# Attention and MLP on one core: batch 0's loads split in the order of use, batch 2's reordering moved up to right behind the GELU pass

## The chip, the cores and the metric

One core of a Trainium2 chip. The time is that of one execution on the device, in microseconds (us); a kernel is compared with the kernel before by runs on the same chip in the same rounds.

## The reference

Softmax attention with one added to the denominator, then a two-layer MLP with exact GELU on its rows:

```python
batch, n_heads, seq, head_dim = (8, 12, 448, 64)
scores = scale * q @ k.T
e = exp(scores - max(scores))
attn = e / (sum(e) + exp(-max) + 1e-09)
x = concat_heads(attn @ v)                 # 3584 rows of 768
h = x @ w_in                               # w_in 768 x 2048
out = (0.5 * h * (1 + erf(h / sqrt(2)))) @ w_out
```

## The kernel before

The kernel works in 48 steps, one for each pair of heads of each batch (6 pairs in a batch). A step makes scores on TensorE, exponentials on ScalarE (ACT), sums of exponentials on VectorE (DVE), then values and denominators on TensorE for a pair one to three steps back. From the seventh step on MLP work of the batch before fills TensorE. GpSimd (POOL) issues all loads but the first four, SyncE (SP) the DMA transposes and most stores.

Queries and keys are needed with head_dim on the partitions. For batches 0 and 1 TensorE transposes them; from batch 2 on DMA does. Batch 2 comes as heads and is first reordered into pairs by VectorE.

```python
raw_pool = ctx.enter_context(tc.tile_pool(name="raw_pool", bufs=2))
ps_bank  = ctx.enter_context(tc.tile_pool(name="ps_bank", bufs=2, space=PSUM))
...
def order_by_pairs(b, w, c0, c1):
    n, nj, raw, name = ((PS, NJ, q_raw, "rawq"), (P, NK, k_raw, "rawk"))[w]
    if b not in ordered[w]:
        ordered[w][b] = raw_pool.tile([n, H, nj, D], FP16, name=name)
    src = raw[b].rearrange("p (c e) j d -> p c e j d", e=2)
    dst = ordered[w][b]...("p (c j e d) -> p c j e d", c=NPAIR, j=nj, e=2)
    for e in range(2):
        nc.vector.tensor_copy(out=dst[:, c0:c1, :, e, :], in_=src[:, c0:c1, e])   # L258
```

The buffers of one name are given out in turn.

```python
def start_step(s):                     # steps 0 to 5
    ...                                # scores, normalize(s - 2)
    transpose_on_pe(0, s + 1)          # pair s + 1 of batch 0
    for c in {NPAIR - 2: (0,), NPAIR - 1: (1, 2, 3)}.get(s, ()):
        transpose_on_pe(1, c)          # batch 1's pairs 0 to 3; pair 4 in step 6
    ...                                # scores of the left-over keys, values, denominators, logarithm
...
step(NPAIR + 1, mlp1(0, 2, 6))
gelu_window(0, 6)
for s in range(NPAIR + 2, NSTEP + 1):
    b, r = divmod(s - 2 - NPAIR, NPAIR)
    ...
        step(s, take(n), ...)          # r == 0: one half of layer 2, evicted by VectorE (osb, L457)
    if b == 0 and r == 0:
        transpose_on_pe(1, NPAIR - 1)  # batch 1's last pair
    fetch(b, r)                        # reordering and DMA transposes
```

Steps count from 0 in the code, so `start_step(0)` is the first step. To evict is to copy a result out of the memory that TensorE writes to (PSUM); `ps_bank` has two such buffers, and a bank is free for the next result only after its eviction.

The softmax here doesn't subtract the row's maximum and nothing guards it: scores larger than these inputs give would overflow.

Of the kernel before, what the change touches and what calls it, by code (L numbers as in the profile page):

```python
# [9 lines left out]
FP32 = mybir.dt.float32  # L10
FP16 = mybir.dt.float16
# [8 lines left out]
def kernel(  # L20
# [9 lines left out]
    nc = tc.nc  # L30

    B, H, S, D = q.shape
    DM = H * D
    DFF = moe_w_in.shape[1]
    P = 128
# [3 lines left out]
    NPAIR = H // 2  # L39
# [4 lines left out]
    LEFT = S % P  # L44
# [7 lines left out]
    shift = math.log(float(S + 1))  # L52

    const = ctx.enter_context(tc.tile_pool(name="const", bufs=1))
# [16 lines left out]
    def load_table(set_id):  # L71
        nc.scalar.add_instruction(  # L72
            mybir.InstLoadActFuncSet(
                name=nc.get_next_instruction_name(),
                act_func_set_id=set_id,
                engine=mybir.EngineType.Activation,
                ins=[],
                outs=[],
            )
        )  # L80
# [6 lines left out]
    kl_raw = [left_pool.tile([P, NPAIR, P], FP16, name=f"klraw{i}") for i in range(2)]  # L87
    vl = [left_pool.tile([P, NPAIR, P], FP16, name=f"vl{i}") for i in range(2)]
    q_raw, k_raw, v_t, qt_t = {}, {}, {}, {}

    def load_heads(tiles, pool, name, src, b, h0=0, h1=H):

        n, nj = (PS, NJ) if src is q else (P, NK)
        if b not in tiles:
            tiles[b] = pool.tile([n, H, nj, D], FP16, name=name)
        nc.gpsimd.dma_start(  # L96
            out=tiles[b][:, h0:h1],
            in_=src[b, h0:h1, 0:n * nj].rearrange("h (p j) d -> p h j d", j=nj),
        )
# [12 lines left out]
    def load_left(tiles, src, b):  # L112
        view = src[b, :, NFULL:S].rearrange("(c e) s d -> e s c d", e=2)
        for e in range(2):
            nc.gpsimd.dma_start(  # L115
                out=tiles[b % 2][e * LEFT:(e + 1) * LEFT, :, e * D:(e + 1) * D], in_=view[e])

    def load_q(b, *heads):
        load_heads(q_raw, raw_pool, "rawq", q, b, *heads)

    def load_k(b, *heads):
        load_heads(k_raw, raw_pool, "rawk", k, b, *heads)

    def load_v(b, *heads):
        load_heads(v_t, v_pool, "vn", v, b, *heads)
# [34 lines left out]
            load_table(SET_LN_EXP)  # L160
    ident = const.tile([P, P], FP16, name="ident")
    make_identity(nc, ident)
    for t in (kl_raw[1], kl_raw[0], vl[0], vl[1]):
        nc.vector.memset(t, 0.0)
    load_left(kl_raw, k, 0)
    load_q(0, 4, 6)
    load_k(0, 4, 6)

    warm = ps_bank.tile([P, 512], FP32, name="bank")
    for _ in range(7):  # L170
        nc.tensor.matmul(
            warm, kl_raw[1][:, 0], kl_raw[1].rearrange("p c x -> p (c x)")[:, 0:512],
            start=True, stop=True)
    ones = const.tile([P, D], FP16, name="ones")
    nc.vector.memset(ones, 1.0)
    ones_left = const.tile([P, P], FP16, name="ones_left")
    nc.gpsimd.memset(ones_left, 0.0)
    for e in range(2):
        r = slice(e * LEFT, (e + 1) * LEFT)
        nc.gpsimd.memset(ones_left[r, e * D:(e + 1) * D], 1.0)  # L180
    expb = const.tile([P, 1], FP32, name="expb")
    nc.vector.memset(expb, -shift)
    oneb = const.tile([P, 1], FP32, name="oneb")
    nc.vector.memset(oneb, math.exp(-shift))

    load_v(0, 0, 6)
    load_left(vl, v, 0)
    load_q(0, 6, 12)
    load_k(0, 6, 12)
    load_v(0, 6, 12)  # L190
    load_q(1)
    load_k(1)
    load_left(kl_raw, k, 1)
# [209 lines left out]
    def layer1(b, fc, direct=False, mid=None):  # L403
        ph = ps_bank.tile([P, 512], FP32, name="bank")
        for m in range(MCH):
            matmul_cols(
                ph[:, 0:S], w_in_sb[:, m, fc * P:(fc + 1) * P], xt_t[b][:, m, :],
                m == 0, m == MCH - 1)
        if mid:
            mid()  # L410
        if direct:
            for c0, c1, dst in gelu_out(b, fc, fc + 1):
                nc.scalar.activation(out=dst[:, 0, :], in_=ph[:, c0:c1], func=AF.Gelu)  # L413
        else:
            if fc == 0:
                h_t[b] = h_pool.tile([P, NBURST, S], FP32, name="hbuf")
            nc.vector.tensor_copy(out=h_t[b][:, fc, :], in_=ph[:, 0:S])  # L417

    def gelu_burst(b, f0, f1):
        for c0, c1, dst in gelu_out(b, f0, f1):  # L420
            nc.scalar.activation(out=dst, in_=h_t[b][:, f0:f1, c0:c1], func=AF.Gelu)
# [15 lines left out]
    def layer2_items(b):  # L437
        if b % 2 == 0:
            tiles = [(gt_even, t * P, [(b, t * P, (t + 1) * P)]) for t in range(NFULL // P)]
        else:  # L440
            tiles = [(gt_odd, 0, [(b - 1, NFULL, S), (b, 0, LEFT)])]
            tiles += [(gt_odd, (t + 1) * P, [(b, LEFT + t * P, LEFT + (t + 1) * P)])
                      for t in range(NFULL // P)]
        halves = []
        for gt, g0, where in tiles:
            def half(nh, mid=None, gt=gt, g0=g0, where=where):

                n0 = nh * NHW
                po = ps_bank.tile([P, 512], FP32, name="bank")
                for fc in range(FCH):  # L450
                    matmul_cols(
                        po[:, 0:NHW], gt[:, fc, g0:g0 + P], w_out_sb[:, fc, n0:n0 + NHW],
                        fc == 0, fc == FCH - 1)
                    if mid and fc == FCH // 2 - 1:
                        mid()
                osb = osb_pool.tile([P, NHW], FP32, name="osb")
                nc.vector.tensor_copy(out=osb, in_=po[:, 0:NHW])  # L457
                r0 = 0
                for bb, c0, c1 in where:
                    store_cols(osb, r0, bb, c0, c1, n0)  # L460
                    r0 += c1 - c0

            for nh in range(NH):
                halves.append((nh if b == 0 else 0, lambda mid=None, nh=nh, half=half: half(nh, mid)))
        return [f for _, f in sorted(halves, key=lambda x: x[0])]
# [75 lines left out]
    def mlp1(b, f0, f1):  # L541
        return [lambda mid=None, fc=fc: layer1(b, fc, mid=mid) for fc in range(f0, f1)]

    def take(n):
        got = l2[:n]
        del l2[:n]
        return got

    def gelu_window(b, n):

        load_table(SET_GELU)
        ready = take(len(l2))
        for f in ready:
            f()
        if not ready:
            for i in range(FCH - n):
                if i < n:
                    gelu_burst(b, i, i + 1)
                layer1(b, n + i, direct=True)
        else:  # L560
            for f0 in range(0, n, n // 2):
                gelu_burst(b, f0, f0 + n // 2)
            for fc in range(n, FCH):
                layer1(b, fc, direct=True)
        load_table(SET_LN_EXP)
        l2.extend(layer2_items(b))
# [34 lines left out]

    def fetch(b, r):

        if r == 0 and b + 2 < B:
            load_v(b + 2)
            load_left(vl, v, b + 2)
        if b == 0 and r in (0, 2):
            c0 = 0 if r == 0 else NPAIR // 2
            for w in range(2):
                order_by_pairs(2, w, c0, c0 + NPAIR // 2)  # L610
                transpose_on_dma(2, w, c0, c0 + NPAIR // 2)
        elif b and r in (0, 1) and b + 2 < B:
            transpose_on_dma(b + 2, r)
        if r == 3 and b + 3 < B:
            load_pairs(q_raw, "rawq", q, b + 3)
            load_pairs(k_raw, "rawk", k, b + 3)
            load_left(kl_raw, k, b + 3)

    step(NPAIR + 1, mlp1(0, 2, 6))
    gelu_window(0, 6)  # L620
    for s in range(NPAIR + 2, NSTEP + 1):
        b, r = divmod(s - 2 - NPAIR, NPAIR)

        half = NBURST // 2
        if b and r < 2:
            step(s, mlp1(b, half * r, half * (r + 1)))
        else:
            left = len(l2) - (0 if b == 0 else 1 if b % 2 == 0 else 2)
            n = left if r == NPAIR - 1 else max(1, left // (NPAIR - r))
            if b and r == 2:  # L630
                n = 2
            step(s, take(n), late=(s == NSTEP or r == (2 if b else 0)))
        if b == 0 and r == 0:
            transpose_on_pe(1, NPAIR - 1)
        fetch(b, r)
        if b and r == 1:
            gelu_window(b, 2 * half)
# [43 lines left out]
```

## Time and profile before

| | |
|---|---|
| time, median | 415.83 us (three runs); 415.61 with a fourth |
| TensorE busy | 400.3 of 414.9 us |
| its idle time from 5 to 40 us | 7.9 us |
| its longest waits for data | 1.7 + 1.1 us (pair 3's queries and keys), 0.7 us (batch 2's transposes) |

TensorE is full from 40 us to near the end, so a change has to take idle time away ahead of that or at 76 us. The lines are in the prediction below. Two marks make runs comparable. One is the table load that opens the first GELU pass on ScalarE, the other the first exponentials of the step near 92 us.

In the timeline of the kernel before (start, length, engine, line, what, then idle time before it and who ended it):

```profile
43.06 1.28 ACT L72 ACT_TABLE_LOAD   x1
...
76.33 0.74 PE L315 MATMUL st<-tqk 64*128 64x448 f16 x6 [0.72 <-DMA tqk<-rawk]
...
92.47 3.33 ACT L305 ACTIVATE et<-st,expb 128x896 f16<-128x896 f32 x4 [2.22 <-PE st L315]
```

The first mark is at 43.06, the second at 92.47, 49.41 us later; the 0.72 us that TensorE waits for batch 2's transposes lie between.

### The profile page before, as it was taken

The numbers are of one execution on the slowest core, as the hardware profiler recorded it, in microseconds if no ns is written. First come the engines' busy times: TensorE is split into PE (matmuls) and PEld (weight loads), VectorE is DVE, ScalarE is ACT, GpSimd is POOL, SyncE is SP. The second block draws the span as 40 slices with busy tenths as digits, with TensorE's granted clock in tenths as the row PEclk, the third lists the DMA queues.
The fourth block names the chain that finished last, engine by engine and source line by source line (L and its number), as shares of the span: only waits on it lengthen the run. The fifth ranks groups of instructions, "written<-read, shape, count | busy, mean of one in ns | idle before, by whom it ended". The sixth has DMA issues, their size and how long they took to land.

```text
span 414.9 us, 10361 instructions
## 1 busy us (share of the span) xinstructions
PE 400.3 (97%) x4403; PEld 249.9 (60%) x4403; DVE 194.8 (47%) x466; ACT 300.5 (72%) x450; POOL 101.5 (24%) x138
## 2 busy tenths in 40 slices
PE   7779999999999999999999999999999999999996
PEld 3345765556656565566555566556565565687785
DVE  5466428773266713674165722576046741540021
ACT  6798879979897757979687766997589676734300
POOL 8631330773523450054300651020000000000000
PEclk9899999999999999999999999999999999999999
DMA  9999999999983997199921999149211100110022
GB/s 154 181 201 202 197 201 178 154 183 162 136 102 67 152 177 65 58 91 140 151 60 44 140 144 118 56 71 136 63 40 42 35 23 20 45 54 20 2 77 76
DMA packets 136638, 43.76 MB, mean 105 GB/s; under 512 B 117712, under 2 KB 136592, under 8 KB 136592
## 3 DMA queue, kind: packets, MB, share of 16 engines
q0 software_dynamic: 91408, 22.39, 57.7%
q1 hardware_dynamic: 43952, 19.60, 29.0%
q10 hardware_dynamic: 1232, 1.11, 0.9%
q8 instruction: 34, 0.56, 0.6%
q14 instruction: 12, 0.10, 0.1%
HBM read 45.61 MB, written 11.01 MB: 136 GB/s over the span
## 4 chain that ended last, share of the span: by engine, by line
PE 88%; DMA 4%; ACT 4%; POOL 2%; DVE 1%; issue 0%
PE bank L224 71%; PE st L315 6%; PE bank L363 6%; DMA tqk<-rawk 3%; ACT et L305 2%; DMA rawk<-in_k_dram 2%; PE st L224 2%; PE st L371 2%; ACT rec L380 1%; ACT rec L383 1%; DVE xt L389 0%; POOL klraw L115 0%; POOL vl L115 0%; POOL rawq L96 0%; ACT L72 0%
## 5 line engine op out<-in xcount | busy, mean ns | idle before, releaser
L305 ACT ACTIVATE et<-st,expb 128x896 f16<-128x896 f32 x192 | 160.3, 914 | 34.7 <-PE st L315 26.0
L224 PE MATMUL bank<-xt,w_in_sb 128*64 128x448 f16 x1536 | 152.4, 353 | 0.2
L224 PEld LDWEIGHTS <-w_in_sb 128*64 128x64 f16 x1536 | 92.8, 110 | 55.6 <-issue 6.3
L457 DVE COPY osb<-bank 128x384 f32<-128x384 f32 x56 | 31.2, 557 | 123.5 <-PE bank L224 123.5
L224 PE MATMUL bank<-w_out_sb,gt_odd 128*64 128x384 f16 x1024 | 88.2, 327 | 0.0
L224 PEld LDWEIGHTS <-gt_odd 128*64 128x64 f16 x1024 | 60.8, 110 | 25.5 <-issue 4.5
L224 PE MATMUL bank<-w_out_sb,gt_even 128*64 128x384 f16 x768 | 68.9, 327 | 0.0
L389 DVE TENSOR_TENSOR xt<-bank,rec 128x448 f16<-128x448 f32 x48 | 29.7, 619 | 64.6 <-PE bank L363 56.0
L224 PEld LDWEIGHTS <-gt_even 128*64 128x64 f16 x768 | 43.6, 110 | 22.9 <-issue 4.4
L413 ACT ACTIVATE gt_odd<-bank 128x448 f16<-128x448 f32 (+1 forms) x74 | 29.1, 394 | 23.0 <-PE bank L224 21.9
L417 DVE COPY hbuf<-bank 128x448 f32<-128x448 f32 x54 | 33.6, 623 | 16.5 <-PE bank L224 15.2
L110 POOL DMA_DIRECT2D rawq<-in_q_dram x40 | 30.7, 783 | 37.2 <-DVE rawq L258 17.0
L315 PE MATMUL st<-tqk 64*128 64x448 f16 x288 | 36.9, 353 | 2.8 <-ACT et L305 1.0
L363 PE MATMUL bank<-et,vn 128*64 128x448 f16 x288 | 36.3, 357 | 0.0
L349 DVE TENSOR_TENSOR ksum<-t,et 128x448 f16<-128x448 f16 x96 | 33.9, 384 | 0.8 <-ACT et L305 0.6
L349 DVE TENSOR_TENSOR t<-et 128x448 f16<-128x448 f16 x96 | 33.2, 388 | 2.1 <-ACT et L305 0.8
L413 ACT ACTIVATE gt_even<-bank 128x384 f16<-128x384 f32 x34 | 16.7, 490 | 22.1 <-PE bank L224 22.1
L349 DVE TENSOR_TENSOR ksum<-ksum,et 64x448 f16<-64x448 f16 x84 | 31.9, 380 | 1.3
L96 POOL DMA_DIRECT2D vn<-in_v_dram x9 | 8.8, 981 | 89.6 <-PE st L315 86.8
L110 POOL DMA_DIRECT2D rawk<-in_k_dram x30 | 24.7, 824 | 20.6 <-DMA rawq<-in_q_dram 19.8
L380 ACT ACTIVATE rec<-st,oneb 128x448 f32<-128x448 f32 x42 | 27.1, 647 | 2.8 <-PE st L371 2.8
L383 ACT ACTIVATE rec<-rec 128x448 f32<-128x448 f32 x48 | 27.6, 577 | 1.5
(57 smaller groups left out, 234.5 us busy)
## 6 DMA issues: line engine op xcount, KB each, us to landing
vn<-in_v_dram POOLq DMA_DIRECT2D x7, 576.0 KB, 10.2
rawq<-in_q_dram POOLq DMA_DIRECT2D x40, 84.0 KB, 11.1
w_in_sb<-in_moe_w_in_dram POOLq DMA_DIRECT2D x4, 768.0 KB, 19.8
w_out_sb<-in_moe_w_out_dram POOLq DMA_DIRECT2D x4, 768.0 KB, 19.8
rawk<-in_k_dram POOLq DMA_DIRECT2D x31, 96.0 KB, 7.4
out_dram<-osb SPq DMA_DIRECT2D x16, 168.0 KB, 2.3
out_dram<-osb SPq DMA_DIRECT2D x16, 144.0 KB, 2.1
out_dram<-osb SPq DMA_DIRECT2D x16, 120.0 KB, 2.0
```

Of the source, the lines that this page charges most:

```text
L110: nc.gpsimd.dma_start(out=dst[:, :, j, e, :], in_=view[j, e])
L224: nc.tensor.matmul(out[x], lhs[:, x], rhs, start=start, stop=stop)
L305: nc.scalar.activation(out=out, in_=in_, func=AF.Exp, bias=expb, scale=scale)
L315: nc.tensor.matmul(st[:, e, 0:S], kt[r, j, :], qt[r], start=True, stop=True)
L349: nc.vector.tensor_tensor(out=dst, in0=a, in1=x, op=ALU.add)
L363: nc.tensor.matmul(po_t[g][e * D:(e + 1) * D, 0:S], v_t[b][:, 2 * c + e, j, :], et[:, 2 * j + e], start=False, stop=(j == NK - 1),)
L380: nc.scalar.activation(out=rec_t[g], in_=den_t.pop(g)[:, 0:S], func=AF.Ln, bias=oneb, scale=1.0)
L383: nc.scalar.activation(out=rec_t[g], in_=rec_t[g], func=AF.Exp, scale=-1.0)
L389: nc.vector.tensor_tensor(out=xt_t[b][:, c, :], in0=po_t.pop(g)[:, 0:S], in1=rec_t.pop(g), op=ALU.mult)
L413: nc.scalar.activation(out=dst[:, 0, :], in_=ph[:, c0:c1], func=AF.Gelu)
L417: nc.vector.tensor_copy(out=h_t[b][:, fc, :], in_=ph[:, 0:S])
L457: nc.vector.tensor_copy(out=osb, in_=po[:, 0:NHW])
```

## The change

It splits batch 0's later loads so that pair 3's queries and keys come alone and first. It starts GpSimd's queue earlier, with a shorter form of warm-up. It moves the reordering of batch 2's first half ahead of the ninth step (s = 8 in the code), so that its DMA transposes go out earlier; the load of batch 2's values is written two steps later.

```diff
-    for t in (kl_raw[1], kl_raw[0], vl[0], vl[1]):
+    nc.vector.memset(ones, 1.0)
+    for t in (kl_raw[0], vl[0], kl_raw[1], vl[1]):
         nc.vector.memset(t, 0.0)
-    nc.gpsimd.memset(ones_left, 0.0)          # and two more
+    nc.vector.memset(ones_left, 0.0)          # and two more
-    for _ in range(7):
-        nc.tensor.matmul(warm, kl_raw[1][:, 0], <512 columns of kl_raw[1]>, ...)
+    for _ in range(54):
+        nc.tensor.matmul(warm[0:D, 0:D], ones, ones, start=True, stop=True)
-    load_v(0, 0, 6)
+    load_v(0, 0, 4)
     load_left(vl, v, 0)
-    load_q(0, 6, 12)
-    load_k(0, 6, 12)
-    load_v(0, 6, 12)
+    load_q(0, 6, 8)
+    load_k(0, 6, 8)
+    load_q(0, 8, 12)
+    load_k(0, 8, 12)
+    load_v(0, 4, 12)
 ...
-        if r == 0 and b + 2 < B:
+        if r == (0 if b else 2) and b + 2 < B:
             load_v(b + 2)
             load_left(vl, v, b + 2)
-        if b == 0 and r in (0, 2):
-            c0 = 0 if r == 0 else NPAIR // 2
+        if b == 0 and r in (-1, 2):
+            c0 = NPAIR // 2 if r == 2 else 0
 ...
     gelu_window(0, 6)
+    fetch(0, -1)
```

More of the change, by code (lines that the diff above doesn't have):

```diff
@@ L162 @@
     make_identity(nc, ident)
-    for t in (kl_raw[1], kl_raw[0], vl[0], vl[1]):
+    ones = const.tile([P, D], FP16, name="ones")
+    nc.vector.memset(ones, 1.0)
+    for t in (kl_raw[0], vl[0], kl_raw[1], vl[1]):
         nc.vector.memset(t, 0.0)
+    ones_left = const.tile([P, P], FP16, name="ones_left")
+    nc.vector.memset(ones_left, 0.0)
+    for e in range(2):
+        r = slice(e * LEFT, (e + 1) * LEFT)
+        nc.vector.memset(ones_left[r, e * D:(e + 1) * D], 1.0)
+    expb = const.tile([P, 1], FP32, name="expb")
+    nc.vector.memset(expb, -shift)
+    oneb = const.tile([P, 1], FP32, name="oneb")
+    nc.vector.memset(oneb, math.exp(-shift))
     load_left(kl_raw, k, 0)
@@ L169 @@
     warm = ps_bank.tile([P, 512], FP32, name="bank")
-    for _ in range(7):
-        nc.tensor.matmul(
-            warm, kl_raw[1][:, 0], kl_raw[1].rearrange("p c x -> p (c x)")[:, 0:512],
-            start=True, stop=True)
-    ones = const.tile([P, D], FP16, name="ones")
-    nc.vector.memset(ones, 1.0)
-    ones_left = const.tile([P, P], FP16, name="ones_left")
-    nc.gpsimd.memset(ones_left, 0.0)
-    for e in range(2):
-        r = slice(e * LEFT, (e + 1) * LEFT)
-        nc.gpsimd.memset(ones_left[r, e * D:(e + 1) * D], 1.0)
-    expb = const.tile([P, 1], FP32, name="expb")
-    nc.vector.memset(expb, -shift)
-    oneb = const.tile([P, 1], FP32, name="oneb")
-    nc.vector.memset(oneb, math.exp(-shift))
-    load_v(0, 0, 6)
-    load_left(vl, v, 0)
-    load_q(0, 6, 12)
-    load_k(0, 6, 12)
-    load_v(0, 6, 12)
+    for _ in range(54):
+        nc.tensor.matmul(warm[0:D, 0:D], ones, ones, start=True, stop=True)
+    load_v(0, 0, 4)
+    load_left(vl, v, 0)
+    load_q(0, 6, 8)
[3 more added lines that the diff above has]
+    load_v(0, 4, 12)
     load_q(1)
```

## The prediction

> **What bounds the kernel now.** I read the page first: busy shares and slices, to see whether there is anything to win and where.
>
> ```profile
> PE 400.3 (97%) x4403; PEld 249.9 (60%) x4403; DVE 194.8 (47%) x466; ACT 300.5 (72%) x450; POOL 101.5 (24%) x138
> ...
> PE   7779999999999999999999999999999999999996
> ...
> PEclk9899999999999999999999999999999999999999
> ```
>
> TensorE is busy 400.3 of 414.9 us, so all its idle time is 14.6 us. The busy time by stretch puts it: about 1.5 us before 5 us, 6.7 from 5 to 30 us (the fourth digit is the last below 9), 1.2 from 30 to 40, 1.1 from 60 to 80, and 4.1 in the last 15 us, which the change doesn't touch. What the change can win is therefore a part of some 9 us, 2.2% of the time; over 2% faster is out of reach. The second thing to see is the clock digit 8 in slice 2 (10.4 to 20.7 us): half speed for about 3 us (finer windows: 0.65 at 16.0 to 16.5, 0.50 from 16.5 to 19.5).
>
> Next, the waits of TensorE:
>
> ```profile
> PE bank L232 <- DMA rawq<-in_q_dram: 1.7, 1, 1.7
> ...
> PE bank L237 <- DMA rawk<-in_k_dram: 1.1, 1, 1.1
> ...
> PE st L315 <- DMA tqk<-rawk: 0.7, 1, 0.7
> ```
>
> The first two are one place: transposes of head pair 3 wait for queries and keys of heads 6 to 11, which come in one load each. The third is batch 2, whose first scores wait for its DMA transposes. The change aims at these. The timeline (start, length, engine, idle before and who ended it) of that place and of the same spot two steps on:
>
> ```profile
> 14.99 0.40 PE L232 MATMUL bank<-ident,rawq 112*64 112x112 f16 x8 [1.69 <-DMA rawq<-in_q_dram]
> 16.52 0.54 PE L237 MATMUL bank<-ident,rawk 128*64 128x128 f16 x6 [1.13 <-DMA rawk<-in_k_dram]
> 17.70 1.34 PE L363 MATMUL bank<-et,vn 128*64 128x448 f16 x6
> 19.77 0.63 ACT L380 ACTIVATE rec<-bank,oneb 128x448 f32<-128x448 f32 x1 [1.56 <-PE bank L224]
> 20.92 3.31 ACT L305 ACTIVATE et<-st,expb 128x896 f16<-128x896 f32 x4
> 25.27 3.31 ACT L305 ACTIVATE et<-st,expb 128x896 f16<-128x896 f32 x4
> ...
> 26.27 0.37 PE L237 MATMUL bank<-ident,rawk 128*64 128x128 f16 x6
> 26.44 0.26 PE L242 MATMUL bank<-ident,klraw 128*64 128x128 f16 x2
> ```
>
> After the wait the values matmuls run at half clock (1.34 us for six here, 0.77 for the same six a step later). Away from the wait ScalarE sets the pace: its steps begin at 20.92 and 25.27, 4.35 us apart, with no idle time.
>
> Last, the loads (from issue to landing, the last figure), asked one by one:
>
> ```profile
> rawq<-in_q_dram POOLq DMA_DIRECT2D x1, 336.0 KB, 7.3
> rawk<-in_k_dram POOLq DMA_DIRECT2D x1, 288.0 KB, 8.1
> vn<-in_v_dram POOLq DMA_DIRECT2D x1, 288.0 KB, 10.1
> rawk<-in_k_dram POOLq DMA_DIRECT2D x1, 576.0 KB, 14.7
> klraw<-in_k_dram POOLq DMA_DIRECT2D x1, 48.0 KB, 14.0
> ```
>
> Issued at 7.64, 8.40, 9.22, 10.97 and 11.97, they land at 14.9, 16.5, 19.3, 25.7 and 26.0; the second klraw load at 26.4. So batch 1's keys and left-over keys land just as TensorE reads them (26.27, 26.44). That is the fact my number hangs on: the queue is full, and a second wait stands right behind the one removed.
>
> **What the Trainium skill says.** "TensorE: Matmul & The Clock Gate", Part 1: the array runs at half clock until busy for a window of about 3.4 us, and falls back after an idle one, the windows running free. The trace agrees: half clock from about 16.4 to 19.5, 3.1 us, after two waits. The same section gives N / 1.2 GHz from start to start of cold matmuls; the 7 warm-up ones of 512 columns fit (3.17 us for all, 0.43 each). "DMA: Bandwidth & Descriptors", Anatomy of one DMA, has a fixed cost of about 2 us for a gpsimd load; the two small loads at 3.42 and 4.08 (3.8 and 3.5 us to landing, some 0.7 of it issue) don't contradict it. Its Specifications want 512 B a descriptor for full rate; the query rows are 512 B, the key and value rows 384, the left-over rows 128, and the queue moves 150 to 210 GB/s here.
>
> **The change part by part.**
>
> 1. Start of GpSimd's queue. The tile that the first left-over load waits for is cleared second of its list instead of after the other: one memset of 0.38 less, less 0.06 for `ones`, so the load starts about 0.3 us earlier than 2.00. The three `ones_left` memsets go from GpSimd to VectorE: the values load starts right after the key load instead of at 5.39 after a stretch of 0.6. In all, values are issued about 0.9 us earlier, and the hole in the traffic at 7 to 8 us (64 against 165 GB/s around it, worth 0.6 us) mostly closes. VectorE's own list ends by about 3.0 us, before its first cast at 4.16.
>
> 2. Warm-up: 54 matmuls of 64 columns for 7 of 512: 3456 columns for 3584, from 1.0 instead of 1.34. At the skill's cold rate an estimate is 54 x 53 ns = 2.9 us, ending near 4; TensorE next works at 4.64. If a weight load doesn't hide behind so short a matmul they take up to twice that and push the start by a microsecond or so. I give nothing for this part.
>
> 3. Order of loads. Before pair 3's keys lie 96+112+96+288+96+336+288 = 1312 KB; after, 96+112+96+192+96+112+96 = 800 KB. 512 KB at about 190 GB/s is 2.7 us, with the earlier start over 3: they land near 13 instead of 16.5, and TensorE asks at 13.3. The wait and the half clock go. ScalarE's step 3 then begins at 13.93 + 4.35 = 18.28 instead of 20.92: 2.64 us won so far. Values of heads 4 to 11 keep the byte count ahead of them, land near 18.7, and are wanted near 19.7: no wait.
>
> 4. What gives it back. Bytes ahead of batch 1's keys and left-overs are the same, so these land earlier only by part 1, which I take as 0.7: 25.7 for the last. TensorE would now ask at 26.44 - 2.64 = 23.8 and wait. From the left-over transposes to the end of the denominators is 28.03 - 26.44 = 1.6 us, so step 4's logarithm can begin at 25.7 + 1.6 = 27.3, against 28.45 before: **1.15 us** remain of 2.64. From there to 60 us all runs on as before, shifted: input weights land at 30.2 to 41.5, against first use at 36.4 and, for the last quarter, about 52.
>
> 5. Batch 2. Four copies (1.00 + 0.80 us of VectorE) move from 62.4 into VectorE's gap between 46.8 and 59.9; their data land at 55.4 and 56.9 before, so the transposes go out at about 56 instead of 63.5. They took 10.4 and 10.6 us to land (73.9 and 76.3); even at 13 they are there by 72. The wait of **0.7** goes. GpSimd's list of operations is the same from here on: values come behind the second half of keys in it either way, so "two steps later" moves no issue. Stores behind the transposes on SyncE's queue come late, but four output buffers cover three steps.
>
> Sum: 1.15 + 0.72 = 1.9 us, from 415.83 to 413.9. I take off little more than a tenth of that for the risks below and say 414.1.
>
> **The rivals.** (a) The second wait takes all: TensorE idles about 2 us near 24, its clock drops as it did at 16.4, and den-to-logarithm takes 2.9 instead of 1.6. For: the same shape of wait did just this. Against: the idle is shorter than the 2.8 before. One chance in four; then only some 0.5 us is won, 415.3. (b) No second wait, since the loads come much earlier: 2.64 + 0.7 = 3.4 us, 412.5. Against: the queue is full from 8 us on. One in seven. (c) The earlier DMA transposes slow batch 2's second-half loads (landing at 67.0 and 69.2, wanted on VectorE at 72.2 and 73.1). Putting the rest of about 0.8 MB ahead of them costs an estimated 2 to 3 us at 200 GB/s, about the margin. VectorE would then hold up the next step by under a microsecond: 414.8. (d) The warm-up is too long or doesn't lift the clock: 1 us lost; one in ten.
>
> **Range and chances.** Center 414.1; (b) gives the low end, 412.6, (a) with (d) the high end, 415.6. The whole idle time in reach (9 us) is just over the 8.3 us that 2% asks, and no part here risks 8 us: faster 0.01, same 0.98, slower 0.01.
>
> **What would show it.** The query and key waits near 14 to 16.5 are gone and the clock stays full there (3); a new wait of TensorE on batch 1's keys or left-over keys near 24 to 25.7, with ScalarE's step 5 at about 28.5 for 29.62 (4); the first DMA transposes issued near 56 and no wait for them at the scores near 75 (5); first scores still near 5.9 (2). Wrong if that second wait is missing or costs the clock, or if VectorE waits for batch 2's second half.

## The result and the profile after

The changed kernel took 416.44 us (median of four, 415.99 to 417.37), against 415.61 before. The ratio is 1.0023, 95% interval 1.0001 to 1.0045. Ratios here are the mean time of one kernel's fast runs over that of the other's of the same rounds, so not quite the ratio of the medians. It is slower by 0.2%, and the predicted range ended at 415.6. The interval only just leaves out 1, and a control with identical code (e8, below) gave nearly as large a ratio, so the loss itself is hardly shown; what is shown is that the predicted win did not come.

The page of the changed kernel, busy shares and slices:

```profile
PE 399.9 (96%) x4450; PEld 252.1 (61%) x4450; DVE 195.5 (47%) x469; ACT 300.5 (72%) x450; POOL 102.3 (25%) x137
...
PE   7789979999999999999999999999999999999996
...
PEclk9999999999999999999999999999999999999999
```

The clock digit 8 is gone (PEclk is the share of full speed granted to TensorE, in tenths), the third slice has 8 for 7, and there is a new 7: slice 6, 51.9 to 62.2 us. The waits of TensorE in the changed kernel (total us, times, longest) name it:

```profile
PE bank L224 <- DVE osb L457: 3.0, 1, 3.0
```

Its timeline shows how it comes about, on VectorE:

```profile
58.50 1.01 DVE L258 COPY rawq<-rawq 112x768 f16<-112x768 f16 x2 [14.43 <-PE bank L232]
59.43 0.80 DVE L258 COPY rawk<-rawk 128x576 f16<-128x576 f16 x2
60.15 0.78 DVE L349 TENSOR_TENSOR ksum<-ksum,et 64x448 f16<-64x448 f16 x2
60.94 0.56 DVE L457 COPY osb<-bank 128x384 f32<-128x384 f32 x1
```

and on TensorE:

```profile
58.06 0.39 PE L232 MATMUL bank<-ident,rawq 112*64 112x112 f16 x8
...
61.64 0.38 PE L224 MATMUL bank<-et,vl 128*64 128x448 f16 x2 [2.96 <-DVE osb L457]
```

VectorE sits idle for 14.43 us in front of the first copy, although the queries are there from about 54.0 us and the keys from 55.6. What ends the wait is the query transposes of batch 1's last pair, which start at 58.06 and take 0.39 us. Only then can the copies run, 1.8 us of them; the sums behind them take 0.8; and the first output eviction, ready since about 57.9, begins at 60.94. TensorE needs the bank that it empties and waits 2.96 us. The wait that the move was to take away did go: the DMA transposes went out at 59.61 and 61.92 us and had landed by 74.7, so TensorE does not wait for them.

The two marks of the changed kernel, and one step in between:

```profile
27.60 3.31 ACT L305 ACTIVATE et<-st,expb 128x896 f16<-128x896 f32 x4
...
41.04 1.28 ACT L72 ACT_TABLE_LOAD   x1
...
92.51 3.33 ACT L305 ACTIVATE et<-st,expb 128x896 f16<-128x896 f32 x4 [2.22 <-PE st L315]
```

The first mark comes at 41.04 for 43.06: 2.02 us won ahead of the GELU pass, in this pair of traces. From there to the second it takes 51.47 us for 49.41: 2.06 us lost. In these two traces the sum is zero. In the medians it is 0.8 us of loss, because the profile of the kernel before had fallen on a slow execution: that execution took 416.62 us, 0.8 to 1.0 over the kernel's median, while the profiled run of the changed kernel (416.6) lies near its own.

### The profile page after: what moved, and what is told of

The parts are those of the page before. It is cut to its first block, busy times and chain, and to the rows that moved or that the text cites. A ratio compares the mean times of both kernels' runs of the same rounds, so it can differ in the third digit from the quotient of the medians.

```text
span 414.8 us, 10457 instructions
## 1 busy us (share of the span) xinstructions
PE 399.9 (96%) x4450; PEld 252.1 (61%) x4450; DVE 195.5 (47%) x469; ACT 300.5 (72%) x450; POOL 102.3 (25%) x137
## 4 chain that ended last, share of the span: by engine, by line
PE 90%; ACT 6%; DVE 2%; DMA 1%; issue 1%; DVEq 0%
PE bank L224 73%; PE st L315 7%; PE bank L363 6%; ACT et L305 4%; PE st L224 2%; PE st L371 2%; DMA hbuf<-in_k_dram 1%; ACT rec L383 1%; ACT rec L380 1%; DVE xt L389 0%; DVE ksum L349 0%; DVE osb L457 0%; PE bank L232 0%; DVE rawk L258 0%; DVE tqk L244 0%
## 5 line engine op out<-in xcount | busy, mean ns | idle before, releaser
L224 PEld LDWEIGHTS <-gt_odd 128*64 128x64 f16 x1024 | 60.6, 110 | 25.7 <-issue 4.5
```

Source lines behind the costliest of these rows:

```text
L224: nc.tensor.matmul(out[x], lhs[:, x], rhs, start=start, stop=stop)
```

## The experiments

Twelve runs in three calls (e1 to e4, e5 to e8, e9 to e12), each on another chip. Times are medians; the kernel before had medians of 415.53, 415.42 and 415.78 us in the three.

| run | what | us | ratio to before | interval | mark 1 | mark 1 to mark 2 |
|---|---|---|---|---|---|---|
| before | | 415.61 | | | 43.06 | 49.41 |
| changed | | 416.44 | 1.0023 | 1.0001 to 1.0045 | 41.04 | 51.47 |
| e1 | change, reordering put back | 417.67 | 1.0042 | 1.0020 to 1.0065 | 40.28 | 53.29 |
| e2 | before, reordering moved | 418.02 | 1.0070 | 1.0042 to 1.0099 | 41.38 | 51.47 |
| e3 | change, last transposes first | 414.40 | 0.9969 | 0.9950 to 0.9988 | 41.02 | 49.54 |
| e4 | change, own buffer | 414.38 | 0.9965 | 0.9943 to 0.9986 | 40.87 | 49.74 |
| e5 | e3, old start | 416.82 | 1.0033 | 1.0010 to 1.0055 | 43.38 | 49.54 |
| e6 | e3, old split | 414.56 | 0.9981 | 0.9961 to 1.0001 | 41.95 | 49.53 |
| e7 | e3, old start and split | 414.61 | 0.9985 | 0.9965 to 1.0005 | 40.72 | 49.54 |
| e8 | before again | 416.14 | 1.0020 | 0.9994 to 1.0046 | 43.07 | 49.50 |
| e9 | change, transposes spread | 413.96 | 0.9968 | 0.9946 to 0.9990 | 40.95 | 48.63 |
| e10 | e9, long warm-up | 414.37 | 0.9971 | 0.9953 to 0.9989 | 41.72 | 48.63 |
| e11 | e5, wait filled | 415.48 | 0.9999 | 0.9982 to 1.0016 | 41.87 | 49.54 |
| e12 | e9, old loads | 414.61 | 0.9972 | 0.9956 to 0.9988 | 41.67 | 48.63 |

Between the marks, kernels with the same late code agree to 0.1 us, with one exception: e1 has the late code of the kernel before and takes 53.29, because its early start runs into the DMA transposes (below). So 49.41 belongs to the kernel before with a late first mark; no trace shows it after an early one. Ahead of mark 1 they don't: the same early code gives 43.06, 43.07, 41.38 and 40.72 (before, e8, e2, e7). The eviction wait of the second half can be read from one trace, what the loads win cannot.

### The two halves of the change alone (e1, e2)

e1, the change with:

```diff
-        if b == 0 and r in (-1, 2):           # and the values at r == 0 again
+        if b == 0 and r in (0, 2):
-    fetch(0, -1)
```

> The change with its reordering of batch 2 put back where it was (start, warm-up and split loads stay). Theory A (the loads win about 2 us and the early reordering loses about 3): 413.6 us, no wait of TensorE on an eviction near 60, its step 5 exponentials at 27.6 as in the changed kernel, and the wait for batch 2's DMA transposes near 75 is there again, up to 0.8 us. Rival B (the 2 us of the start are lost again anyway, later in the loads): 415.6.

e2 is the kernel before with the opposite edit.

> The kernel before with only the reordering moved behind the GELU pass. Theory A: TensorE waits about 3 us for the first output eviction near 63, the waits of 0.7 and 0.4 us near 76 and 62 go; 415.6 + 3.0 - 1.1 = 417.5 us. Rival B (the reordering is harmless by itself): 415 us.

e2 did what theory A said, with the same wait of 3.0 us and the same 51.47 us between the marks as the changed kernel; the moved reordering makes this loss by itself (2.06 us between the marks, 2.5 us in the medians). e1 missed both theories: 417.67, slower than either kernel. It reaches mark 1 early, at 40.28, and then waits for the transposes far longer than 0.8 us. In e1, the issue of the key transposes on SyncE's queue:

```profile
62.89 4.27 SPq L265 DMA_TRANSPOSE tqk<-rawk  x1
```

the time from that issue to landing, in the view of its DMA:

```profile
tqk<-rawk SPq DMA_TRANSPOSE x1, 12.9
```

and TensorE's timeline there:

```profile
75.79 0.83 PE L315 MATMUL st<-tqk 64*128 64x448 f16 x6 [2.95 <-DMA tqk<-rawk]
76.55 2.77 PE L224 MATMUL bank<-w_out_sb,gt_even 128*64 128x384 f16 x16
```

The same two views of the kernel before:

```profile
65.69 4.53 SPq L265 DMA_TRANSPOSE tqk<-rawk  x1
```

```profile
tqk<-rawk SPq DMA_TRANSPOSE x1, 10.6
```

Issued 2.8 us earlier, the transposes land 0.5 us earlier (75.8 for 76.3) and take 12.9 us for 10.6. The likely reason is that they now run longer beside loads that were still in flight and had not moved as much: the second half's keys land at 68.4 (69.2 in the kernel before), batch 2's values at 74.7 (74.4). No run tests this alone. So what the loads win at the start is waited for again here, and more, since the clock then falls: in e1 it is 0.50 from 76.5 to 79.5, and the 16 matmuls of the last line take 2.77 us, for 1.49 in the kernel before. By this trace the loads' half needs the earlier transposes; that was the intent of the second half.

### What the copies wait for (e3, e4)

e3 takes TensorE's transposes of batch 1's last pair ahead:

```diff
     step(NPAIR + 1, mlp1(0, 2, 6))
+    transpose_on_pe(1, NPAIR - 1)
     gelu_window(0, 6)
     fetch(0, -1)
-        if b == 0 and r == 0:
-            transpose_on_pe(1, NPAIR - 1)
```

> The change, with TensorE's transposes of batch 1's last pair taken ahead of the GELU pass, so that the reordering's target buffer is free before. Theory A (the copies wait for that buffer): the copies start when their data land, near 54 to 55.5, the 3 us wait goes, 412.7 us. Rival C (the copies are late because their data or VectorE are late, or they are too long where they stand): the wait of TensorE stays at 1 to 3 us, 414 to 416 us.

e4 leaves them where they were and gives the first half's reordered queries and keys a buffer of their own, a tile of the pool that held the GELU's input:

```diff
-            ordered[w][b] = raw_pool.tile([n, H, nj, D], FP16, name=name)
+            spare["half"] = h_pool.tile([P, 2 * NBURST * S], FP16, name="hbuf")   # first half
```

(A third buffer in the pool itself did not fit in memory.)

> The change, with the first half's reordered copy in a buffer of its own (free since the GELU pass) and the transposes of batch 1's last pair left where the change has them. Theory A: the same 412.7 us as the run before, as only the buffer's wait is taken away. Rival C: 414 to 416 us. A third theory, D (it is TensorE's order and not the buffer): only the run before wins, this one stays at 416.

Both win the 2 us: 414.40 and 414.38, under the kernel before by 0.3%, and in neither does TensorE wait for the eviction. (By time alone they would also fit rival C's 414 to 416; the wait that is gone decides. In e3 the first copy starts at 54.28, released by the landing of its queries.) e4's VectorE:

```profile
54.94 1.01 DVE L265 COPY hbuf<-rawq 112x768 f16<-112x768 f16 x2 [11.03 <-ACT gt_odd L422]
56.43 0.81 DVE L265 COPY hbuf<-rawk 128x576 f16<-128x576 f16 x2 [0.48 <-DMA rawk<-in_k_dram]
57.16 0.79 DVE L358 TENSOR_TENSOR ksum<-ksum,et 64x448 f16<-64x448 f16 x2
57.99 0.56 DVE L466 COPY osb<-bank 128x384 f32<-128x384 f32 x1
...
72.19 0.81 DVE L265 COPY rawk<-rawk 128x576 f16<-128x576 f16 x2 [1.14 <-DMA rawk<-in_k_dram]
```

The copies are over by 57.2 and the eviction begins at 57.99 instead of 60.94. As e4 changes only where these copies go, the wait was the buffer's; theories C and D fall. The instruction list of the built kernel had said so: its first copy waits for two DMA semaphores and for TensorE, and in e3 the last is gone.

```
changed:  L258 TensorCopy rawq<-rawq 112x12x64 [waits DMASW4_49,DMASW3_49,PE_49]
e3:       L258 TensorCopy rawq<-rawq 112x12x64 [waits DMASW4_49,DMASW3_49]
```

By the code, the buffers named `rawq` go in turn to batch 0, batch 1, batch 2 and the reordered batch 2: the last takes over batch 1's. The query copies write columns 0 to 1535 of the buffer and the transposes still to come read 2560 to 3071: the wait covers the whole buffer though the parts don't overlap.

The expected 412.7 was missed by 1.7 us. In e3 the transposes cost 0.9 us where they now stand, before a GELU pass in which TensorE has no idle time (the pass takes 14.99 us for 14.07). In e4 the last line above is the prediction's rival (c): the second half's keys come 1.14 us too late for VectorE, and TensorE waits 0.86 us.

### Start and split, with the fault mended (e5, e6, e7, e8)

On e3, the start (clearing, warm-up, `ones_left` on GpSimd), the split loads, or both, as in the kernel before:

```diff
 e5:  start as before          e6:  load_v(0, 0, 6), load_q(0, 6, 12), ... as before
 e7:  both                     e8:  the kernel before, unchanged
```

> The mended kernel (transposes of batch 1's last pair first; 414.4 us) with the start of the kernel before: its order of clearing, ones_left on GpSimd, 7 warm-up matmuls of 512 columns. Theory S (the new start costs: the left-over load, some 0.35 us earlier, runs beside the first query and key loads, and the first exponentials come at 6.2 to 7.0 for 6.1 to 6.3): 413.9 us, first exponentials at 6.3 or before. Rival: the start is worth nothing either way, 414.4; or its earlier loads are needed, then a wait for loads between 13 and 25 us and 415.

> The mended kernel with the loads of batch 0 as before (6 heads and 6 heads). Theory S2 (the split is what takes the wait at pair 3 away): the waits on queries and keys near 14 to 16 us are there, the step from the third to the fourth exponentials is 5.5 to 7.0 us in place of 4.35, and the time is 1.2 to 2.6 us over 414.4: 415.6 to 417. Rival (the earlier start of GpSimd's queue does it without the split): 414.4 us and no such wait.

> The kernel before with only batch 2's reordering behind the GELU pass and the transposes of batch 1's last pair ahead of it. If the parts add: 414.4 minus 0.5 of the start plus 1.2 to 2.6 of the split = 415.1 to 416.5 us. If batch 2's DMA transposes, and not the first loads, set the time of the kernel before: 414 us or less, as they are issued 6 us earlier here.

> The kernel before, unchanged, for a second profile and as a control: ratio 1.000 within 0.2%. Theory V (the profile that the prediction read fell on a slow run, 416.6 for a median of 415.6): the wait at pair 3 here is under the 2.8 us of that profile, nearer 1.5, and the exponentials after the GELU pass begin near 57 for 58.4. Rival: the same 2.8 us and 58.4.

Most of these expectations missed. Theory S fell: the old start is not faster but loses 2.4 us when combined with the split. The last case of its rival, a wait for loads and 415 us, came true in kind, at more than its size. e7 has the old start too and differs from e5 in the split alone: 414.61 for 416.82. So the split without the new start does harm. Theory S2 fell too: e6 and e7, with the unsplit loads, have no long step at pair 3 (4.35 and 4.36 us from the third to the fourth step's exponentials, for 6.99 in the profile of before) and take 414.6. That is the time of e6's rival and between e7's two expectations. (e6's trace has half clock from 7.0 to 14.2 us, which made its first steps late; the keys had landed when TensorE asked for them.) e8 came out as the rival to theory V said, the same slow picture a second time (43.07), again in a profiled run, 416.65, that is above its median. Its ratio of 1.0020 for identical code says how far to trust a ratio here, though its interval holds 1.

e5 shows the prediction's second wait, which the changed kernel's trace did not have:

```profile
23.78 0.40 PE L234 MATMUL bank<-ident,rawq 112*64 112x112 f16 x8 [0.65 <-DVE xt L391]
25.23 0.54 PE L239 MATMUL bank<-ident,rawk 128*64 128x128 f16 x6 [1.05 <-DMA rawk<-in_k_dram]
25.55 0.65 PE L244 MATMUL bank<-ident,klraw 128*64 128x128 f16 x2
...
26.64 1.43 PE L365 MATMUL bank<-et,vn 128*64 128x448 f16 x6
```

Batch 1's keys were issued at 12.25 us here (10.97 in the kernel before) because the split puts two more loads of some 0.7 us each ahead of them on GpSimd. They landed at 25.2, and at 23.7 in the changed kernel, and with 1.05 us of waiting the clock is at half from about 25.2 to 28.5 (six values matmuls take 1.43 us for 0.77). ScalarE's step takes 6.97 us instead of 4.35. In e7, TensorE waited just as long for pair 3's keys, and the clock did not fall:

```profile
13.99 0.40 PE L232 MATMUL bank<-ident,rawq 112*64 112x112 f16 x8 [0.28 <-DMA rawq<-in_q_dram]
15.52 0.36 PE L237 MATMUL bank<-ident,rawk 128*64 128x128 f16 x6 [1.13 <-DMA rawk<-in_k_dram]
...
16.14 0.74 PE L363 MATMUL bank<-et,vn 128*64 128x448 f16 x6
```

There the six values matmuls take 0.74 us, for 1.34 in the profile of before, and ScalarE's next step comes on time, 4.36 us later. The last wait is the same, 1.13 us, but not what stood ahead of it: from the last scores to the next matmul that is not a transpose, TensorE's idle time adds up to 1.4 us in e7 and 1.2 in e12 (clock full), 1.7 in e2, 1.9 in e5 and 2.8 in before and e8 (clock fell). Six traces don't fix a threshold.

### Is it the wait or the clock? (e11)

On e5, six matmuls that nobody reads stand between the query and the key transposes:

```diff
+            if (b, c) == (1, 0):
+                idle = ps_bank.tile([P, 512], FP32, name="bank")
+                for _ in range(6):
+                    nc.tensor.matmul(idle, kl_raw[0][:, 5], <512 columns of kl_raw[0]>, ...)
```

> The kernel with the old start and the split loads (416.8 us, TensorE 1 us idle for batch 1's keys at 24 us, then half clock to 28.5), with 6 matmuls of 512 columns between the query and the key transposes there, whose result nobody reads. Theory H (the clock that falls in that wait costs, more than the wait): no half clock between 25 and 28.5 us, the sixth step's exponentials begin within 5 us of the fifth's for 7.0, and the time falls to 415.3 or less. Rival (the late keys themselves cost it): it stays at 416.8, or over it.

```profile
24.11 1.46 PE L239 MATMUL bank<-klraw 128*128 128x512 f16 x6 [0.17 <-DVE tqk L252]
25.50 0.36 PE L245 MATMUL bank<-ident,rawk 128*64 128x128 f16 x6
...
26.13 0.74 PE L371 MATMUL bank<-et,vn 128*64 128x448 f16 x6
```

The key transposes begin even later than in e5 (25.50 for 25.23), but the clock stays full, the values take 0.74 us, the step 5.68 us for 6.97, and the median falls from 416.82 to 415.48. (I had expected a step under 5 us and 415.3 or less; both missed, the time by 0.2. The keys landed at 24.5 in this trace, but their transposes, behind the filler, still start later.) That speaks for theory H: of the 2.6 us that such a wait costs, about half goes with the clock. It isn't strict: the two were timed in different calls, and the intervals of their ratios overlap.

### A better place for the transposes, and the warm-up (e9, e10, e12)

e9 is the change with batch 1's transposes spread over the earlier steps:

```diff
-        for c in {NPAIR - 2: (0,), NPAIR - 1: (1, 2, 3)}.get(s, ()):
+        for c in {NPAIR - 2: (0, 1), NPAIR - 1: (2, 3, 4)}.get(s, ()):
-    transpose_on_pe(1, NPAIR - 2)
+    transpose_on_pe(1, NPAIR - 1)
-        if b == 0 and r == 0:
-            transpose_on_pe(1, NPAIR - 1)
```

> The change with batch 1's transposes spread so that none is left after the GELU pass: pairs 0 and 1 in the fifth step, 2 to 4 in the sixth, 5 where 4 was. Theory A: the copies find their buffer free as in the mended kernel (414.4 us), and TensorE does these transposes where ScalarE sets the pace, so that the 0.9 us that they cost ahead of the GELU pass are won too: 413.5 us; from the table load of the GELU pass to the exponentials near 90 us 48.6 us for 49.5. Rival: the transposes delay the logarithms of the sixth step by as much, 414.4.

> The run before with the warm-up of 7 matmuls of 512 columns (on the second cleared tile) in place of 54 of 64. Theory W (the short matmuls end 0.7 us before TensorE's first work and the clock falls back in the first 14 us, as in 4 of 5 traces with them and none of 5 without): no half clock before 14 us, and 0.3 us faster than the run before, 413.2. Rival: no difference, half clock there as well.

> Start, warm-up and loads of the kernel before, with the reordering behind the GELU pass and the transposes spread as in the first run of these four. What it lacks against that run is the whole of the loads' part of the change. Theory L (the loads win 1.2 us where nothing later takes it back): 414.7 for 413.5. Rival (they win nothing in the median, only in the slow draws): within 0.3 us of it.

e9 is the best kernel, 413.96 us, ratio 0.9968. Between the marks it takes the 48.6 us expected, 0.78 less than the kernel before in its two traces. It gives some of it back in the fifth step, which grows from 4.35 to 4.98 us with one more transpose, so 413.5 was not reached. e10 refutes theory W: with the long warm-up it is no faster. Nor is the half clock of the first microseconds peculiar to the short one; e12 has the old warm-up, and its first six scores took 1.30 us, as in the changed kernel, against 0.83 in the profile of before. e12 against e9 is the loads' worth with everything else mended: 0.65 us in the medians, 0.2 us in the ratios. e7 against e3 gives 0.2 us and 0.7 us. By the median e12 lies between theory L (1.2 us) and its rival (at most 0.3), by the ratio with the rival. The loads win something under a microsecond, which these rounds don't separate from nothing.

## Why the prediction was wrong

**Part 5, the step that failed.** "Four copies (1.00 + 0.80 us of VectorE) move from 62.4 into VectorE's gap between 46.8 and 59.9; their data land at 55.4 and 56.9 before, so the transposes go out at about 56". It asked when the data come and not when the target is free. The copies wait for the buffer until 58.5, and as VectorE takes its list in order, the first eviction, ready at 57.9, waits behind them until 60.94. In place of 0.72 us won, 2.06 us were lost (51.47 for 49.41 between the marks): a difference of 2.8 us to the sum. The transposes went out near 60, not 56, though that was early enough for the 0.72 us to go. e2 shows the loss alone, e3 and e4 that it is the buffer. With the wait mended the kernel takes 414.40 and 414.38, against the predicted 414.1. Part of that nearness is luck: between the marks e3 (49.54) wins nothing over 49.41, because the transposes cost 0.9 us elsewhere. Only e9, with 48.63, shows a win of the size that part 5 gave.

**Part 4, what the loads win, is not confirmed.** It expected 1.15 us, left over by a second wait from 2.64. The traces of one pair gave 2.02, but 2.64 itself was read from a slow execution; in the medians and ratios the loads win 0.2 to 0.7 us, which is not clear of noise. The changed kernel had no second wait: batch 1's keys landed at 23.7, 2 us earlier than in the profile of before, where the prediction had allowed 0.7. It had counted the bytes ahead of them, but not the two more loads that GpSimd must issue: they went out at 11.30 us, later than before (10.97), in spite of the earlier start. With the new start and the split they landed at 23.3 to 24.1 us in six traces (changed, e1, e3, e4, e9, e10), with the new start and the loads unsplit at 22.4 (e6). With the old start and the loads unsplit it was 25.7, 25.7, 23.8, 23.6 and 24.0 us (before, e8, e2, e7, e12): no later in three of five than with the change. Why these five fall into two groups some 2 us apart is open.

**Rival (a)** was real, but not in this kernel: e5 has just that wait and that fall of the clock. **Rival (c)** was seen in e4, at the size given. **Rival (d)**, the warm-up, left no sign in e10.

**Part 3** held in what it says of the wait: every trace with the split has 4.35 us from the third to the fourth exponentials, where unsplit loads gave 6.99, 6.86, 5.48, 4.36, 4.35 and 4.35 (before, e8, e2, e7, e12, e6). It takes away a wait that only some executions pay for.

**Part 1** held for the issues (the left-over load at 1.65 for 2.00, values at 4.44 for 5.39), and e5 shows that the split needs them. **Part 2**: the 54 matmuls took 3.09 us, ending at 4.08. The first scores came at 6.38 us, for 5.9 as the sign of this part, but with the same warm-up they came at 5.67 in e9; nothing that the runs show came of it either way.

**The later load of the values** moved no issue, as said: it went out at 52.84 us for 54.10, in the same place of GpSimd's list. No run tries it alone.

**Slips in the working.** The last slice of TensorE below 9 is the third, not the fourth. The half clock of the profile lasts 3.4 us (16.1 to 19.6 in windows of 0.1 us), not 3.1. And rivals (a) and (d) together give 415.3 + 1 = 416.3, not the 415.6 at which the range ends.

**What was left out.** The prediction took one profile as the kernel. The profiled run was 416.62 for a median of 415.83, and the 0.8 us between was worth as much as the terms of the sum.

## What to carry to other kernels

Before an instruction is moved ahead on an in-order engine, look at all that it waits for, the target's buffer as well as the data; whatever stands behind it in the queue waits with it, and a reader of the old buffer may be on another engine. A transfer issued earlier into a busy queue may land earlier by much less: the first key transposes of batch 2, against the kernel before, went out 2.8 us earlier in e1 and landed 0.5 us earlier; in e9 it was 8.1 and 5.4 us. Splitting a load also costs issues, which delay what stands behind it in the same queue (e5). And compare the profiled run's time with the median before pricing a wait by it.

## What the Trainium skill lacked or had wrong

- "TensorE: Matmul & The Clock Gate", Part 1, has the clock fall after an idle window of about 3.4 us. Here it fell with TensorE idle at most 1.05 us in one piece and 1.9 us in all since its last scores (e5, half clock from 25.2 to 28.5), and not in another wait of 1.1 us, 1.4 in all (e7).
- The same page, Part 1, gives N / 1.2 GHz for cold matmuls, but none for 64 columns with a weight load each: 54 took 3.09 us, 57 ns each for the 53 worked out from it, so the weight loads hid.
- "DMA: Bandwidth & Descriptors", Latency and other measured facts, gives a transpose rate of 261 GB/s. It does not say what transposes cost beside a full queue of gpsimd loads: the same key transposes took 10.6 us to land when issued at 65.7, 12.9 when issued at 62.9.
- No page warns that the same loads can land 2 us apart from one execution to another: batch 1's keys at 23.6 to 25.7 us with the same early loads.
